# The first layer's high part of g: rounded by ScalarE in place of GpSimd

## The chip, the core and the metric

The kernel runs on one core of a Trainium2 chip. The time is the device time of one execution in microseconds; the core's engines are TensorE (PE, with PEld for its weight loads), VectorE (DVE), ScalarE (ACT), GpSimd (POOL) and SyncE (SP, which issues the DMAs). Each engine takes its own instructions in order and waits on semaphores for the others. The profile is one execution taken by the hardware profiler; its times count from the first instruction.

## The reference

Three parts follow one another: an attention in which a query sees only the keys of its own cluster, a dense layer (the first layer below), and a layer of four experts mixed by given probabilities (the second). The change lies in the first layer, on 1536 tokens:

```python
def _moe_ref(x, w_in, w_out):            # x [1536, 512], w_in [512, 2048], w_out [2048, 512]
    h = x @ w_in
    g = np.where(h > 0.0, h, 1.0 * (np.exp(np.minimum(h, 0.0)) - 1.0))
    return (g @ w_out).astype(np.float32)
```

`w_in` and `w_out` come in 64-bit floats; the kernel turns them into 32-bit ones itself.

## The kernel before

Every matrix product of the first layer is three matmuls of fp32r operands: a value x is split into a high part xh, which is x rounded to fp32r, and a low part xl = x - xh, and the products hh, hl and lh are summed in PSUM.

The layer is cut into 48 steps. A step takes one block of 512 tokens (`tb`, three of them) and one chunk of 128 of the 2048 columns of `w_in` (n, sixteen of them). The chunks form groups of 2, 4, 5 and 5; a group goes through all its chunks for one token block, then for the next. A step has two halves:

- `emit_G1(s)`: 12 matmuls (L745) make `h` in one of two PSUM buffers. ScalarE takes `r` = relu(-h) (L752) and exp(-r) (L753), VectorE joins them to `gg` (L754), and GpSimd splits `gg`: `gh` is its high part (L755), `gl` the low one (L756). `r` and `gg` have two buffers, `gh` and `gl` four.
- `emit_G2(s)`: 12 matmuls (L915) multiply `gh` and `gl` by the chunk's rows of `w_out` and add into four PSUM tiles `a`, of five buffers. At the end of a group the four tiles go to `acc` in SBUF: in the first group by four copies of ScalarE (L931), later by additions on VectorE (L933). The next step's second to fourth tile need the buffers that these free.

G1 runs two steps ahead of G2 (`LAG`): the program's order is G1(s+2), G2(s), G1(s+3), and so on. With G1(s+2) written before G2(s), the exp of step s+2 stands ahead of the L931 of step s in ScalarE's queue.

Between the two halves a clock of ticks moves generators on that load and split the weights of later chunks (`w_split`). A chunk takes from the 64-bit words: ScalarE L702 (absolute value of the high word) and L708 (its sign), VectorE L704, L707 and L710 (clamp, shift, join the words), ScalarE L714, VectorE L716 (the sign put back), ScalarE L718 (`wh`, the high part), GpSimd L721 (`wl`, the low part). L702 of one chunk waits until GpSimd has finished L721 of the chunk two before, whose buffer it takes. Chunks 0 and 1 are split during the attention, chunks 2 to 15 in the first layer; the last steps of the layer split what the second layer needs. In the second layer GpSimd has no work on `g`.

No line but one is touched; it stands in `emit_G1`.

Of the kernel before, what the change touches and what calls it, by code (L numbers as in the profile page):

```python
# [13 lines left out]
AF = mybir.ActivationFunctionType  # L14
ALU = mybir.AluOpType
# [31 lines left out]
def kernel(  # L47
# [14 lines left out]
    pe, act, dve, pool, sp = nc.tensor, nc.scalar, nc.vector, nc.gpsimd, nc.sync  # L62
# [661 lines left out]
    def moe():  # L724
# [10 lines left out]
        def emit_G1(s):  # L735
            ly, tb, n = steps[s][:3]
            if ly == 2:
                return
            wh, wl = w_t[n]
            ps = ps_h.tile([128, 512], F32, tag=f"h{s % 2}", name="h")  # L740
            for kk in range(KD):
                f = slice(kk * 128, (kk + 1) * 128)
                xh, xl = xT[tb][kk][:, 0], xT[tb][kk][:, 1]
                for i, (w, x) in enumerate(((wh, xh), (wh, xl), (wl, xh))):
                    pe.matmul(  # L745
                        ps, lhsT=w[:, 0, f], rhs=x, start=(kk == 0 and i == 0), stop=(kk == KD - 1 and i == 2)
                    )
            gh = gp.tile([128, 512], F32R, tag="gh", name="gh")
            gl = gp.tile([128, 512], F32R, tag="gl", name="gl")
            r = tp.tile([128, 512], F32, tag="r", name="r")  # L750
            gg = tp.tile([128, 512], F32, tag="gg", name="gg")
            act.activation(out=r, in_=ps, func=AF.Relu, scale=-1.0)  # L752
            act.activation(out=r, in_=r, func=AF.Exp, scale=-1.0)  # L753
            dve.scalar_tensor_tensor(out=gg, in0=r, scalar=-1.0, in1=ps, op0=ALU.add, op1=ALU.max)  # L754
            pool.tensor_scalar(gh, gg, 1.0, 0.0, ALU.mult, ALU.add)  # L755
            pool.tensor_tensor(gl, gg, gh.bitcast(F32), ALU.subtract)  # L756
            g_t[s] = [(gh, gl)]

# [238 lines left out]
        for s in range(-LAG, NS):  # L997


            nxt = s + (1 if s >= NS1 else LAG)  # L1000
            q = None
            if s < NS1:
                tick(2 * s)
            if nxt < NS1:
                emit_G1(nxt)
            elif nxt < NS and s != NS1 - 1:
                ready(nxt)
                q = quad_early(nxt)
            if s >= 0:
                emit_G2(s, (0,) if q else range(4))  # L1010
            if s < NS1:
                tick(2 * s + 1)
            if q:
                quad_late(nxt, *q)
                if s >= NS1:
                    tick(2 * s, 3)
                    tick(2 * s + 1, 2)
                emit_G2(s, (1, 2, 3))
            g_t.pop(s, None)
            if s == 12:  # L1020
                probs()
# [33 lines left out]
```

## Time and profile before

| | |
|---|---|
| three runs | 1055.17, 1059.05 (median), 1060.33 us |
| profiled execution, its time | 1059.59 us |
| its span, first to last instruction | 1057.9 us |
| granted TensorE clock, mean | 0.994 |
| busy: PE, DVE, ACT, POOL | 1033.5, 734.3, 525.0, 392.6 us |
| `gh` on POOL (L755), 48 instructions | 40.7 us, 849 ns each (615 to 1606) |
| `gl` on POOL (L756), 48 | 73.0 us, 1520 ns each (1286 to 2343) |
| `wl` on POOL (L721), 14 | 39.2 us, 2799 ns each |

The attention ends near 274 us, the first layer runs from there to 538 us, the second layer to the end. The mean times of GpSimd's instructions hide a spread: one shape takes anything between the two ends given. A clock of 1 is 2.4 GHz, 0.5 is 1.2 GHz. Busy matmuls overlap, so that a busy TensorE is told by the absence of idle time, not by its share.

### The profile page before, as it was taken

The page shows a single profiled execution, that of the slowest core. Times are in us where ns is not written, and L with a number is a line of the kernel's source. Part 1 is how long each engine was busy: PE and PEld are TensorE (multiplying, and loading weights), DVE is VectorE, ACT ScalarE, POOL GpSimd, SP SyncE. Part 2 cuts the span into 40 slices and gives each one's busy share as a digit, 9 for nine tenths or more (in the row PEclk, how much of TensorE's full clock was granted, in tenths as well). Part 3 has the DMA queues.
Part 4 walks back from the last instruction along what each step waited for, and adds up shares of the span by engine and source line. Part 5 has one row for each costly group of instructions (what it writes and reads, how often), then busy time and mean ns, then how long its engine had stood idle before and what let it go on. Part 6 is the DMA issues. An engine that isn't in the chain of part 4 may idle for free.

```text
span 1057.9 us, 16441 instructions
## 1 busy us (share of the span) xinstructions
PE 1033.5 (98%) x6253; PEld 922.4 (87%) x6253; DVE 734.3 (69%) x1248; ACT 525.0 (50%) x1081; POOL 392.6 (37%) x394
## 2 busy tenths in 40 slices
PE   7999999999989999999999999999999999999998
PEld 6999999989867888888888989898989898989897
DVE  6898999898658866244677666767666667666665
ACT  4889999888667654233443332333332333332331
POOL 2778888979568757353643000000000000000000
PEclk9899999999999999999999999999999999999999
DMA  7747554430332322010002001111011111011003
GB/s 176 170 119 162 129 126 119 125 89 7 118 118 83 118 79 82 0 40 1 1 1 81 11 30 40 41 40 40 6 36 40 40 41 40 3 38 41 1 1 120
DMA packets 61789, 67.53 MB, mean 64 GB/s; under 512 B 29008, under 2 KB 47440, under 8 KB 61712
## 3 DMA queue, kind: packets, MB, share of 16 engines
q1 hardware_dynamic: 61712, 66.49, 22.1%
q8 instruction: 49, 0.80, 0.3%
q14 instruction: 28, 0.23, 0.1%
HBM read 43.08 MB, written 3.15 MB: 44 GB/s over the span
## 4 chain that ended last, share of the span: by engine, by line
PE 81%; DVE 7%; POOL 4%; ACT 4%; issue 2%; SPq 1%; DMA 1%; POOLq 0%; ACTq 0%; DVEq 0%
PE a L915 35%; PE h L765 23%; PE h L745 10%; PE x L441 4%; PE tps L412 3%; PE s L364 2%; PE s L367 2%; POOL p L400 1%; DVE pl L433 1%; DVE nm L373 1%; SPq L228 1%; DVE wa L710 1%; DMA KB<-kh 1%; ACT e L382 1%; POOL wl L721 1%
## 5 line engine op out<-in xcount | busy, mean ns | idle before, releaser
L765 PEld LDWEIGHTS h<-x,w1op 128*128 128x128 f32 x2016 | 257.4, 190 | 10.2 <-ACT r L776 1.2
L765 PE MATMUL h<-x,w1op 128*128 128x256 f32 x2016 | 261.2, 285 | 1.0 <-ACT r L776 1.0
L915 PE MATMUL a<-w2op,gh 128*128 128x512 f32 x768 | 238.4, 392 | 0.0
L915 PEld LDWEIGHTS a<-w2op,gh 128*128 128x128 f32 x768 | 138.1, 188 | 23.8
L924 DVE SCALAR_TENSOR_TENSOR acc<-a,prob,acc 128x512 f32<-128x512 f32 x180 | 129.7, 747 | 40.1 <-PE a L915 40.1
L915 PE MATMUL a<-w2op,gl 128*128 128x512 f32 x384 | 149.8, 390 | 0.0
L745 PE MATMUL h<-xT,wh 128*128 128x512 f32 x384 | 119.0, 391 | 1.5 <-DVE gg L754 1.5
L400 POOL TENSOR_SCALAR p<-e,sm 128x768 f32<-128x768 f32 x96 | 88.4, 927 | 43.8 <-DVE sm L394 29.6
L754 DVE SCALAR_TENSOR_TENSOR gg<-r,h 128x512 f32<-128x512 f32 x48 | 32.9, 685 | 103.0 <-ACT r L753 81.5
L373 DVE TENSOR_REDUCE nm<-s 128x1 f32<-128x768 f32 x96 | 90.9, 947 | 4.3 <-PE s L367 4.1
L382 ACT ACTIVATE e<-s,nm 128x768 f32<-128x768 f32 x96 | 86.6, 902 | 3.9 <-POOL p L400 2.5
L412 PE MATMUL tps<-ident,p 128*128 128x128 f32 x576 | 85.3, 281 | 2.9 <-DVE pl L433 2.8
L745 PEld LDWEIGHTS h<-xT,wh 128*128 128x128 f32 x384 | 72.2, 189 | 17.3 <-DVE gg L754 2.3
L915 PEld LDWEIGHTS a<-w2op,gl 128*128 128x128 f32 x384 | 72.1, 188 | 15.7
L776 ACT ACTIVATE r<-h 128x256 f32<-128x256 f32 x48 | 18.4, 384 | 134.8 <-PE h L765 134.8
L433 DVE TENSOR_TENSOR pl<-tps,ph 128x512 fp32r<-128x512 f32 x112 | 76.2, 683 | 8.1 <-ACT ph L425 6.7
L915 PE MATMUL a<-gh,wh 128*128 128x512 f32 x192 | 75.5, 393 | 3.4 <-ACT acc L931 3.4
L441 PE MATMUL x<-ph,v 128*128 128x256 f32 x288 | 76.5, 297 | 1.4 <-DVE xs L461 1.3
L755 POOL TENSOR_SCALAR gh<-gg 128x512 fp32r<-128x512 f32 x48 | 40.7, 849 | 97.7 <-DVE gg L754 95.9
L915 PE MATMUL a<-gl,wh 128*128 128x512 f32 x192 | 75.4, 393 | 0.0
L915 PE MATMUL a<-gh,wl 128*128 128x512 f32 x192 | 75.2, 392 | 0.0
L745 PE MATMUL h<-xT,wl 128*128 128x512 f32 x192 | 74.8, 389 | 0.0
(152 smaller groups left out, 1900.3 us busy)
## 6 DMA issues: line engine op xcount, KB each, us to landing
st<-in_moe_w_dram SPq DMA_DIRECT2D x32, 512.0 KB, 4.3
st<-in_moe_w_in_dram SPq DMA_DIRECT2D x14, 512.0 KB, 3.7
st<-in_moe_w_out_dram SPq DMA_DIRECT2D x14, 512.0 KB, 4.6
QA<-qh SPq DMA_DIRECT2D x32, 192.0 KB, 4.0
nq<-in_q_dram SPq DMA_DIRECT2D x16, 192.0 KB, 3.8
nk<-in_k_dram SPq DMA_DIRECT2D x16, 192.0 KB, 3.8
nv<-in_v_dram SPq DMA_DIRECT2D x8, 384.0 KB, 4.1
QB<-ql SPq DMA_DIRECT2D x16, 192.0 KB, 4.2
```

Of the source, the lines that this page charges most:

```text
L373: dve.tensor_reduce(out=m_t[w][:, i:i + 1], in_=s_t[HALF * w + i][:, :, 0:384], axis=AX.XY, op=ALU.max, negate=True)
L382: act.activation(out=e, in_=s_t.pop(u)[:, :, 0:384], func=AF.Exp, bias=m_t[w][:, i:i + 1], accum_out=e_t[w][0][:, i:i + 1])
L400: pool.tensor_scalar(p, e_t[w][1 + i].rearrange("p a b -> p (a b)"), e_t[w][0][:, i:i + 1], 1.0, ALU.mult, ALU.mult)
L412: pe.transpose(ps[:, x, :], p_t[w][i][:, c * 128:(c + 1) * 128], ident)
L433: dve.tensor_tensor(out=l, in0=ps, in1=h.bitcast(F32), op=ALU.subtract)
L441: pe.matmul(x_t[w], lhsT=v2[j][:, r, c, :], rhs=t[:, :, c, :], start=(c == 0 and t is ph[w]), stop=(c == T - 1 and t is pl[w]),)
L745: pe.matmul(ps, lhsT=w[:, 0, f], rhs=x, start=(kk == 0 and i == 0), stop=(kk == KD - 1 and i == 2))
L754: dve.scalar_tensor_tensor(out=gg, in0=r, scalar=-1.0, in1=ps, op0=ALU.add, op1=ALU.max)
L755: pool.tensor_scalar(gh, gg, 1.0, 0.0, ALU.mult, ALU.add)
L765: pe.matmul(ps, lhsT=w[wz][kk], rhs=x[xz][:, kk], start=(start and kk + i == 0), stop=(stop and kk == 1 and i == 2), skip_group_check=True,)
L915: pe.matmul(ps, lhsT=x, rhs=y, start=(opens and i == 0), stop=(closes and i == len(ops) - 1))
L924: dve.scalar_tensor_tensor(out=t, in0=ps, scalar=pr, in1=t, op0=ALU.mult, op1=ALU.add)
```

## The change

ScalarE makes `gh` by a copy whose output type rounds; GpSimd keeps the subtraction. Both engines write the same tile from the same `gg`.

```diff
             act.activation(out=r, in_=ps, func=AF.Relu, scale=-1.0)
             act.activation(out=r, in_=r, func=AF.Exp, scale=-1.0)
             dve.scalar_tensor_tensor(out=gg, in0=r, scalar=-1.0, in1=ps, op0=ALU.add, op1=ALU.max)
-            pool.tensor_scalar(gh, gg, 1.0, 0.0, ALU.mult, ALU.add)
+            act.activation(out=gh, in_=gg, func=AF.Copy)
             pool.tensor_tensor(gl, gg, gh.bitcast(F32), ALU.subtract)
```

The order of the other instructions on every engine is the same before and after. On TensorE and VectorE nothing moves at all; on ScalarE 48 instructions come in, on GpSimd as many go.

ScalarE around the first L931, before (wh_4498 is the high part of chunk 3; L702 here belongs to chunk 4):

```order
L714 ACTIVATE wa<-wa 128x1024
L702 ACTIVATE wa<-st 128x1024
L752 ACTIVATE r<-h 128x512
L753 ACTIVATE r<-r 128x512
L931 ACTIVATE acc<-a 128x512 x4
L708 ACTIVATE wsg<-st 128x1024
L718 ACTIVATE wh_4498<-wa 128x1024
```

and with the change:

```order
L714 ACTIVATE wa<-wa 128x1024
L702 ACTIVATE wa<-st 128x1024
L752 ACTIVATE r<-h 128x512
L753 ACTIVATE r<-r 128x512
L755 ACTIVATE gh<-gg 128x512
L931 ACTIVATE acc<-a 128x512 x4
L708 ACTIVATE wsg<-st 128x1024
L718 ACTIVATE wh_4498<-wa 128x1024
```

The copy of the newest step has come between its exp and the four copies into `acc` of an older step.

ScalarE around the third L931, with the change (wh_4646 is the high part of chunk 5):

```order
L755 ACTIVATE gh<-gg 128x512
L708 ACTIVATE wsg<-st 128x1024
L718 ACTIVATE wh_4646<-wa 128x1024
L752 ACTIVATE r<-h 128x512
L753 ACTIVATE r<-r 128x512
L755 ACTIVATE gh<-gg 128x512
L931 ACTIVATE acc<-a 128x512 x4
L714 ACTIVATE wa<-wa 128x1024
```

The two L755 are new, the other rows stood there in this order before.

## Rows read from the trace of the kernel before

**Rows 1.** Busy by stretch: PE, PEld, DVE, ACT, POOL; PEclk, DMA, GB/s.
```profile
276.00:330.00 54.00, 49.10 (x204) 38.45 (x203) 35.66 (x31) 37.76 (x51) 33.87 (x22) 0.97 0.28 98
...
330.00:538.00 208.00, 208.00 (x919) 172.24 (x918) 119.76 (x136) 93.61 (x133) 126.57 (x95) 1.00 0.14 46
```

**Rows 2.** TensorE by time: start, length, operation; idle before, what ended it.
```profile
296.48 0.50 PE L915 MATMUL a<-gh,wh 128*128 128x512 f32 x1 [2.54 <-ACT acc L931]
...
317.92 0.74 PE L745 MATMUL h<-xT,wh 128*128 128x512 f32 x2 [0.91 <-DVE gg L754]
...
322.83 0.50 PE L915 MATMUL a<-gh,wh 128*128 128x512 f32 x1 [0.87 <-ACT acc L931]
...
325.69 0.73 PE L745 MATMUL h<-xT,wh 128*128 128x512 f32 x2 [0.55 <-DVE gg L754]
```

**Rows 3.** Busy by stretch, as rows 1 (PEclk third from the end).
```profile
296.48:303.00 6.52, 6.52 (x21) 5.22 (x22) 6.45 (x5) 4.64 (x7) 5.87 (x3) 0.74 0.00 0
```

**Rows 4.** The other three engines by time, 282 to 296 us.
```profile
282.75 0.67 DVE L754 SCALAR_TENSOR_TENSOR gg<-r,h 128x512 f32<-128x512 f32 x1
...
282.86 1.06 ACT L714 ACTIVATE wa<-wa 128x1024 f32<-128x1024 f32 x1 [1.55 <-DVE wa L710]
...
286.27 0.58 ACT L752 ACTIVATE r<-h 128x512 f32<-128x512 f32 x1
...
286.88 0.63 ACT L753 ACTIVATE r<-r 128x512 f32<-128x512 f32 x1
...
286.94 0.69 DVE L707 TENSOR_SCALAR wa<-wa 128x1024 int32<-128x1024 int32 x1
...
287.42 1.04 ACT L718 ACTIVATE wh<-wa 128x1024 fp32r<-128x1024 f32 x1
...
287.62 0.69 DVE L754 SCALAR_TENSOR_TENSOR gg<-r,h 128x512 f32<-128x512 f32 x1
...
288.23 1.22 DVE L710 SCALAR_TENSOR_TENSOR wa<-st,wa 128x1024 int32<-128x1024 int32 x1
...
288.40 1.53 POOL L755 TENSOR_SCALAR gh<-gg 128x512 fp32r<-128x512 f32 x1 [2.05 <-DVE gg L754]
...
290.01 1.29 POOL L756 TENSOR_TENSOR gl<-gg,gh 128x512 fp32r<-128x512 f32 x1
...
291.25 2.39 POOL L721 TENSOR_TENSOR wl<-wa,wh 128x1024 fp32r<-128x1024 f32 x1
...
293.68 1.12 ACT L702 ACTIVATE wa<-st 128x1024 f32<-128x1024 f32 x1 [3.14 <-POOL wl L721]
...
295.85 2.04 ACT L931 ACTIVATE acc<-a 128x512 f32<-128x512 f32 x4
```

**Rows 5.** ScalarE by time: a copy of 128x512 from SBUF to SBUF.
```profile
500.54 0.62 ACT L833 ACTIVATE x<-xs 128x512 fp32r<-128x512 f32 x1
```

**Rows 6.** The three engines by time, 319 to 325 us.
```profile
319.03 1.17 ACT L708 ACTIVATE wsg<-st 128x1024 f32<-128x1024 f32 x1 [1.96 <-DVE wa L716]
...
320.06 1.67 DVE L707 TENSOR_SCALAR wa<-wa 128x1024 int32<-128x1024 int32 x1
...
320.11 1.04 ACT L718 ACTIVATE wh<-wa 128x1024 fp32r<-128x1024 f32 x1
...
321.23 2.73 POOL L721 TENSOR_TENSOR wl<-wa,wh 128x1024 fp32r<-128x1024 f32 x1
...
321.76 3.28 DVE L710 SCALAR_TENSOR_TENSOR wa<-st,wa 128x1024 int32<-128x1024 int32 x1
...
322.19 2.04 ACT L931 ACTIVATE acc<-a 128x512 f32<-128x512 f32 x4
...
324.96 0.68 DVE L754 SCALAR_TENSOR_TENSOR gg<-r,h 128x512 f32<-128x512 f32 x1
```

**Rows 7.** ScalarE and VectorE by time, 308 to 318 us.
```profile
308.60 2.04 ACT L931 ACTIVATE acc<-a 128x512 f32<-128x512 f32 x4
...
317.17 0.69 DVE L754 SCALAR_TENSOR_TENSOR gg<-r,h 128x512 f32<-128x512 f32 x1 [6.62 <-ACT r L753]
```

## Prediction

> **What bounds the kernel now.** I read the busy time by stretch first. From 330 to 538 us, most of the first layer, TensorE is busy for all 208.00 us, while ScalarE is busy for 93.61 and GpSimd for 126.57: whatever moves between those two is covered there by matmuls, and costs nothing unless a step's ScalarE work outgrows the step [rows 1]. In the layer's opening, 276 to 330 us, TensorE is busy for 49.10 of 54.00 us [rows 1]. The missing 4.9 us are four waits in TensorE's rows: 2.54 before 296.48 and 0.87 before 322.83, both ended by the first copies into `acc` (L931), and 0.91 before 317.92 and 0.55 before 325.69, both ended by `gg` (L754) [rows 2]. The first wait also costs clock: over the 6.52 us from 296.48 to 303.00 the granted clock averaged 0.74 (it fell to half, 1.2 of 2.4 GHz, for part of it), so 0.26 x 6.52 = 1.7 us of work was lost [rows 3]. The change can only count in this opening, where ScalarE, VectorE and GpSimd split the weights of chunks 2 to 5 and work on `g` at once.
>
> **The change, part by part.** Removed: 48 copies on GpSimd; the one at 288.40 took 1.53 us [rows 4]. Added: 48 on ScalarE. The trace has a ScalarE copy of the same size and type, SBUF to SBUF: 0.62 us [rows 5]. Over 48 that is 30 us. Behind 330 us it lies under the matmuls, in the 208.00 - 93.61 = 114 us in which ScalarE is idle [rows 1]; if that cover were gone, each step would pay up to 0.62 + 0.69 (the wait for `gg`). Moved: nothing on TensorE, VectorE or the DMA queue (the loads of the weights only follow L710, which frees their buffers). But there is a new wait. ScalarE's `gh` needs `gg`, which VectorE makes after ScalarE's exp (L753). ScalarE, which takes its queue in order, thus stands still for `gg` (0.69) and then copies (0.62): everything queued behind comes 0.69 + 0.62 + 0.04 of hand-overs = 1.35 us later, later still if VectorE is late. What stands behind is L714, L718 (the weights) and, three times, L931, for which TensorE waits.
>
> One more thing from the rows: VectorE's operations on the weights and GpSimd's hold each other up. L710 took 1.22 us when it ran from 288.23 [rows 4], but 3.28 when GpSimd's `wl` ran from 321.23 to 323.96: it ended 1.08 after it [rows 6]. I treat them as taking turns, whoever asked first. `gg`, which reads PSUM, I take as free of this.
>
> I carry the rows forward to the three L931.
>
> *First.* `gg` of step 1 ends at 282.75 + 0.67 = 283.42; the copy behind it ends at 284.0, so L714 moves from 282.86 to 284.0 (+1.1) [rows 4]. The chunk's L716 and L708 and then step 2's L752 follow, the latter from 286.27 to 287.5 (+1.2) [rows 4]. `gg` of step 2 then ends at 289.5, its copy at 290.1, and L718 moves from 287.42 to 290.0, ending 291.05 [rows 4]. On GpSimd `gh` is gone, but `gl` must let L710 (1.22, from 289.5) pass: 290.7 + 1.29 = 292.0; `wl` 2.39 more: 294.4, against 291.25 + 2.39 = 293.64 [rows 4]. So the 1.53 taken off GpSimd is eaten up by the wait for L718, and `wl` is 0.7 late. L702 waits for it (293.68 to 294.4), L752 and L753 follow, and then the new `gg` and `gh` before L931: 295.85 + 0.7 + 1.35 = 297.9 [rows 4]. TensorE comes back about 2.05 us later, near 298.5.
>
> *Second.* The L931 at 308.60 moves by some 1.9 in the same way [rows 7]; TensorE, itself 2.05 late, meets it without a new wait. The L718 behind it is late by as much, but GpSimd is rid of `gh`, so `wl`, L702, L752 and `gg` at 317.17 come some 1.1 late: the latter ends at 319.0 [rows 7]. TensorE would have been there at 317.92 - 0.91 + 2.05 = 319.1. The 0.91 is swallowed, and its lag is 1.1 [rows 2].
>
> *Third.* Here the queue matters most. Before, L931 at 322.19 did not need the `gg` of its step, which ran only at 324.96 because VectorE stood in L710 [rows 6]. Now the copy of that `gg` stands ahead of L931. From 319.0: VectorE's L716 (1.2, as L710 of the same size) to 320.2; GpSimd's `gl` (1.29) to 321.5; L704 and L707 (0.6 to 0.7 each, as L707 alone took 0.69 [rows 4]) to 322.75. ScalarE after L716: L708 1.17, L718 1.04, ready at 322.4 [rows 6], so `wl` asks while L707 runs and goes first: 2.39, to 325.1; L710 ends 1.08 later at 326.2; `gg` 326.9; `gh` 327.5; the first L931 0.6 later, 328.1. TensorE restarts there instead of at 322.83: +5.3, after a wait of about 5.4 us [rows 2]. The 0.55 wait that followed falls away: lag 4.7.
>
> *Clock.* Nothing before shows so long a wait. Below: the waits of 0.87 and 0.91 left no such trace, so 0. Above: the 2.54 us wait cost 1.7 [rows 3]. 5.4 is nearer the latter, so I take 1.7. Behind 330 us TensorE has no wait to give the time back with [rows 1].
>
> Sum: 4.7 + 1.7 = 6.4 us. The profiled execution took 1059.59 (span 1057.9 and 1.7 around it), so 1066.0. The median of the three runs, 1059.05, lies 0.5 below the profiled execution, which is no more than the runs differ among themselves.
>
> **The rivals.**
> - *L710 goes first at the third place.* The margin in the sum is 0.35 us (322.4 against 322.75). Then L710 ends at 324.0, `gg` 324.7, `gh` 325.3, and TensorE restarts at 325.9: +3.1, less 0.55, plus 1.7 of clock: 4.25 us, 1063.8. For it: a small shift of ScalarE's L718 suffices. Against: at 321.23 the same turn fell to `wl` before [rows 6].
> - *A second drop, or the first one longer.* If the first wait, 4.6 instead of 2.54, cost another 1.7, and this lag were not swallowed at 317.92: 1067.7. For it: the longer the wait, the more the clock may fall [rows 3]. Against: at the second place TensorE waits for the other engines anyhow.
> - *Nothing comes of it.* If VectorE and GpSimd hinder each other less than I say, `wl` and L710 overlap, `gg` at the third place comes near 323.5, the lag stays under about 1.5 and there is no clock drop: 1059.6 to 1061.
> - *Faster.* GpSimd's `gh` no longer takes turns with VectorE: in the opening each copy takes up to 1.53 us out of their common time [rows 4]. If ScalarE's wait for `gg` is absorbed, the weights come sooner, and up to 4.9 us of waits and 1.7 of clock could go: 1053 at best, some 1056 likely. It decides if `wl` ends before 293.64 in spite of the later L718; in my sum it ends 0.7 after. The Trainium skill ("SBUF — State Buffer", section "Who interferes with whom") has the mechanism: a VectorE instruction with two SBUF inputs, or in a two-port mode, and a GpSimd instruction reading SBUF exclude each other for a whole instruction, and ScalarE never waits on anyone. By that page alone, moving a copy from GpSimd to ScalarE relieves a lock and should gain; the trace agrees on the lock (3.28 against 1.22), but the page's rule says nothing of ScalarE's queue.
>
> **How the numbers follow.** My forecast, `wl` first at the third place, gets 0.50 and 1066.0; L710 first 0.20 (1063.8); more clock lost 0.07 (1067.7); nothing 0.17 (1060); faster 0.06 (1056). Some 0.5%, 5.3 us, is what a measurement of this kernel tells from no change, so from 1059.6 the line lies at 1064.9. The forecast with 6.4 is barely over it, and about a fifth of its chance falls under; of L710 first a sixth falls over. Slower: 0.40 + 0.03 + 0.07 = 0.50; faster: 0.06; same: the rest, 0.44. The range takes in all of the two first cases, the upper end of "nothing" and most of the lost clock: 1060 to 1068.5.
>
> **What would show it.** In the profile after: `gh` on ScalarE near 0.62; at the first wait `acc` ending TensorE's idle time near 298.5 with over 4 us; no wait on `gg` near 319; a wait of 3 to 5.5 us for the third L931, with `gg` of that step just ahead of `gh`; half clock behind it; no TensorE wait from 335 to 538. The prediction is wrong if the third L931 comes within 1.5 us of TensorE's need, if `wl` comes sooner than before, or if waits arise behind 335 us, where I count none.

## The result, and the profile after

With the change the kernel takes 1068.01 us (median of five runs, 1064.69 to 1068.75), before it 1059.83 beside them: the ratio is 1.0075, with a 95% interval of 1.005 to 1.010. It is slower, by about 8 us. The profiled execution took 1068.1, its span 1066.3.

The page's first part, busy time by engine:

```profile
PE 1035.4 (97%) x6253; PEld 924.6 (87%) x6253; DVE 725.1 (68%) x1248; ACT 552.9 (52%) x1129; POOL 346.3 (32%) x346
```

The move itself is as announced: GpSimd lost 46 us and 48 instructions, ScalarE gained 28 us and 48. The group of the new line, with its idle time:

```profile
L755 ACT ACTIVATE gh<-gg 128x512 fp32r<-128x512 f32 x48 | 30.4, 633 | 48.6 <-DVE gg L754 48.6
```

So each copy takes 0.63 us and ScalarE stands still for `gg` 1.0 us ahead of it on average: the wait costs ScalarE more than the work. The stretches of [rows 1], and a later one that ends 2 us behind the first layer's new end at 543.78 (PE, PEld, DVE, ACT, POOL; PEclk, DMA, GB/s):

```profile
276.00:330.00 54.00, 44.90 (x181) 36.19 (x180) 28.23 (x27) 38.16 (x54) 21.75 (x13) 0.92 0.28 95
330.00:538.00 208.00, 208.00 (x916) 172.16 (x915) 112.19 (x132) 116.73 (x170) 89.88 (x54) 1.00 0.14 47
340.00:546.00 206.00, 205.37 (x912) 170.12 (x910) 112.09 (x134) 112.90 (x167) 87.99 (x55) 1.00 0.13 44
```

TensorE is idle for 9.1 of 54 us in the opening, against 4.9 in [rows 1]; the middle is still covered; 0.6 us is lost near 546. TensorE's rows at the waits, answering to [rows 2]:

```profile
298.51 0.80 PE L915 MATMUL a<-gh,wh 128*128 128x512 f32 x1 [4.44 <-ACT acc L931]
...
327.85 0.67 PE L915 MATMUL a<-gh,wh 128*128 128x512 f32 x1 [4.66 <-ACT acc L931]
...
546.45 0.74 PE L765 MATMUL h<-x,w1op 128*128 128x256 f32 x4 [1.08 <-ACT r L776]
```

Two waits of [rows 2] have grown (2.54 to 4.44, 0.87 to 4.66), two are gone (0.91, 0.55), and one at the end of the layer is new. The clock behind the two long ones, answering to [rows 3]:

```profile
298.51:305.00 6.49, 6.49 (x17) 5.13 (x18) 4.23 (x4) 5.70 (x9) 3.85 (x3) 0.57 0.27 77
327.85:335.00 7.15, 7.15 (x24) 5.76 (x25) 3.63 (x5) 6.29 (x10) 1.90 (x2) 0.76 0.35 128
```

It fell to half behind both, 1.2 of 2.4 GHz for part of the stretch. The first and third place on the other engines, where [rows 4] and [rows 6] show them before:

```profile
287.55 0.58 ACT L752 ACTIVATE r<-h 128x512 f32<-128x512 f32 x1
...
289.62 0.63 ACT L755 ACTIVATE gh<-gg 128x512 fp32r<-128x512 f32 x1 [0.82 <-DVE gg L754]
290.15 1.05 ACT L718 ACTIVATE wh<-wa 128x1024 fp32r<-128x1024 f32 x1
...
291.83 2.40 POOL L721 TENSOR_TENSOR wl<-wa,wh 128x1024 fp32r<-128x1024 f32 x1
...
294.26 1.12 ACT L702 ACTIVATE wa<-st 128x1024 f32<-128x1024 f32 x1 [2.11 <-POOL wl L721]
...
297.88 2.04 ACT L931 ACTIVATE acc<-a 128x512 f32<-128x512 f32 x4
...
322.51 2.46 POOL L721 TENSOR_TENSOR wl<-wa,wh 128x1024 fp32r<-128x1024 f32 x1 [1.03 <-PE h L745]
...
322.79 3.25 DVE L710 SCALAR_TENSOR_TENSOR wa<-st,wa 128x1024 int32<-128x1024 int32 x1
...
325.97 0.68 DVE L754 SCALAR_TENSOR_TENSOR gg<-r,h 128x512 f32<-128x512 f32 x1
...
326.68 0.63 ACT L755 ACTIVATE gh<-gg 128x512 fp32r<-128x512 f32 x1 [3.11 <-DVE gg L754]
327.22 2.04 ACT L931 ACTIVATE acc<-a 128x512 f32<-128x512 f32 x4
```

At the third place one reads the chain from below: TensorE waits for L931, L931 stands behind `gh`, `gh` waited 3.11 us for `gg`, and `gg` stands behind an L710 that took 3.25 us beside GpSimd's `wl`.

At the layer's end (ScalarE and VectorE, 541 to 547 us):

```profile
541.98 1.51 DVE L660 TENSOR_TENSOR T<-st 128x256 f32<-128x256 f32 x1
543.41 0.41 DVE L661 TENSOR_TENSOR T<-st 128x256 f32<-128x256 f32 x1
543.75 0.68 DVE L754 SCALAR_TENSOR_TENSOR gg<-r,h 128x512 f32<-128x512 f32 x1
...
544.46 0.64 ACT L755 ACTIVATE gh<-gg 128x512 fp32r<-128x512 f32 x1 [1.94 <-DVE gg L754]
545.00 0.61 ACT L833 ACTIVATE x<-xs 128x512 fp32r<-128x512 f32 x1
545.51 0.61 ACT L645 ACTIVATE w1op<-st 128x512 fp32r<-128x512 f32 x1
546.03 0.36 ACT L776 ACTIVATE r<-h 128x256 f32<-128x256 f32 x1
```

The same pattern once more: the last `gh` waits 1.94 us for a `gg` behind VectorE's other work, and ScalarE comes to L776, the second layer's first relu, without a pause and too late for TensorE. In the trace of before it had idled there for 1.13 us:

```profile
537.23 0.62 ACT L645 ACTIVATE w1op<-st 128x512 fp32r<-128x512 f32 x1
538.98 0.38 ACT L776 ACTIVATE r<-h 128x256 f32<-128x256 f32 x1 [1.13 <-PE h L765]
```

**A ledger.** Single runs of one kernel differ by some 5 us, so I add up profiled executions by stretch: the first layer (first L745 to first L765), the second (to the end of the last matmul), and the rest of the span. Before 264.03 + 515.89 + 3.95, after 269.62 + 517.52 + 5.00: +5.59, +1.63, +1.05, together 8.3, against 8.5 between the two profiled times (1068.1 - 1059.59). Two marks go further into the opening: when TensorE begins G2 of step 6, ahead of the third place (46.78 us after the first L745 before, 48.19 after), and G1 of step 10, behind it (57.31 and 62.90). From there to the layer's end both need 206.72 us.

### The profile page after: what moved, and what is told of

It reads as the page before. It is cut to its first block, busy times and chain, and to the rows that moved or that the text cites. A ratio compares the mean times of both kernels' runs of the same rounds, so it can differ in the third digit from the quotient of the medians.

```text
span 1066.3 us, 16427 instructions
## 1 busy us (share of the span) xinstructions
PE 1035.4 (97%) x6253; PEld 924.6 (87%) x6253; DVE 725.1 (68%) x1248; ACT 552.9 (52%) x1129; POOL 346.3 (32%) x346
## 4 chain that ended last, share of the span: by engine, by line
PE 80%; DVE 7%; ACT 5%; POOL 3%; issue 3%; SPq 1%; DMA 0%; ACTq 0%; POOLq 0%; DVEq 0%
PE a L915 34%; PE h L765 23%; PE h L745 9%; PE x L441 4%; PE tps L412 4%; PE s L364 2%; PE s L367 2%; DVE pl L433 1%; POOL p L400 1%; DVE nm L373 1%; ACT e L382 1%; POOL wl L721 1%; ACT ph L425 1%; PE lps L240 1%; PE lps L239 1%
## 5 line engine op out<-in xcount | busy, mean ns | idle before, releaser
L765 PEld LDWEIGHTS h<-x,w1op 128*128 128x128 f32 x2016 | 257.5, 190 | 11.8 <-ACT r L776 2.8
L765 PE MATMUL h<-x,w1op 128*128 128x256 f32 x2016 | 261.6, 285 | 2.2 <-ACT r L776 2.1
L915 PE MATMUL a<-w2op,gh 128*128 128x512 f32 x768 | 238.4, 392 | 0.0
L915 PEld LDWEIGHTS a<-w2op,gh 128*128 128x128 f32 x768 | 138.1, 188 | 23.9
L915 PE MATMUL a<-w2op,gl 128*128 128x512 f32 x384 | 149.8, 390 | 0.0
L745 PE MATMUL h<-xT,wh 128*128 128x512 f32 x384 | 118.9, 391 | 0.0
L756 POOL TENSOR_TENSOR gl<-gg,gh 128x512 fp32r<-128x512 f32 x48 | 67.4, 1403 | 149.2 <-ACT gh L755 141.7
L754 DVE SCALAR_TENSOR_TENSOR gg<-r,h 128x512 f32<-128x512 f32 x48 | 32.9, 686 | 102.6 <-ACT r L753 102.5
L776 ACT ACTIVATE r<-h 128x256 f32<-128x256 f32 x48 | 18.4, 383 | 134.0 <-PE h L765 134.0
L745 PEld LDWEIGHTS h<-xT,wh 128*128 128x128 f32 x384 | 72.6, 189 | 15.3
L915 PEld LDWEIGHTS a<-w2op,gl 128*128 128x128 f32 x384 | 72.1, 188 | 15.6
L915 PE MATMUL a<-gh,wh 128*128 128x512 f32 x192 | 76.3, 398 | 9.1 <-ACT acc L931 9.1
L915 PE MATMUL a<-gl,wh 128*128 128x512 f32 x192 | 76.1, 397 | 0.0
L915 PE MATMUL a<-gh,wl 128*128 128x512 f32 x192 | 76.0, 396 | 0.0
L745 PE MATMUL h<-xT,wl 128*128 128x512 f32 x192 | 75.0, 390 | 0.0
```

The source lines that it names most:

```text
L745: pe.matmul(ps, lhsT=w[:, 0, f], rhs=x, start=(kk == 0 and i == 0), stop=(kk == KD - 1 and i == 2))
L765: pe.matmul(ps, lhsT=w[wz][kk], rhs=x[xz][:, kk], start=(start and kk + i == 0), stop=(stop and kk == 1 and i == 2), skip_group_check=True,)
L915: pe.matmul(ps, lhsT=x, rhs=y, start=(opens and i == 0), stop=(closes and i == len(ops) - 1))
```

## Experiments

All numbers in one table (us; the marks count from the first L745; the end is the span, which the profile gives to a tenth, less the end of the last matmul). "Before" was run beside each, with medians of 1059.03 to 1059.41; the recorded ratio is not exactly the quotient of the two medians.

| | median | ratio, 95% interval | first layer | second | end | G2(6) | G1(10) |
|---|---|---|---|---|---|---|---|
| before | 1059.83 | | 264.03 | 515.89 | 3.95 | 46.78 | 57.31 |
| the change | 1068.01 | 1.0075 [1.0050, 1.0100] | 269.62 | 517.52 | 5.00 | 48.19 | 62.90 |
| E1 steps below 10 | 1065.22 | 1.0045 [1.0028, 1.0062] | 269.63 | 516.19 | 3.96 | 48.11 | 62.91 |
| E2 steps from 10 | 1061.86 | 1.0027 [1.0018, 1.0037] | 264.05 | 517.24 | 5.05 | 46.77 | 57.33 |
| E3 steps 3, 5, 7 | 1063.87 | 1.0037 [1.0023, 1.0051] | 269.23 | 515.91 | 3.89 | 46.63 | 62.51 |
| E4 all but 3, 5, 7 | 1063.21 | 1.0030 [1.0014, 1.0046] | 265.49 | 517.53 | 5.00 | 48.47 | 58.77 |
| E5 step 7 | 1065.11 | 1.0059 [1.0040, 1.0078] | 269.12 | 516.18 | 3.93 | 46.74 | 62.40 |
| E6 step 3* | 1058.74 | 1.0003 [0.9979, 1.0027] | 262.90 | 516.18 | 3.93 | 46.75 | 56.17 |
| E7 fillers | 1066.41 | 1.0070 [1.0039, 1.0100] | 268.06 | 517.52 | 5.07 | 47.95 | 61.34 |
| E8 all but the last 3 | 1065.93 | 1.0066 [1.0029, 1.0104] | 270.83 | 516.19 | 4.19 | 47.95 | 64.11 |
| E9 tiny copies* | 1056.02 | 0.9992 [0.9974, 1.0010] | 264.06 | 515.91 | 3.88 | 46.78 | 57.34 |
| E10 third buffer | 1053.85 | 0.9958 [0.9944, 0.9972] | 258.60 | 515.90 | 3.91 | 42.45 | 51.88 |
| E11 change, third buffer* | 1062.02 | 1.0028 [1.0012, 1.0044] | 266.56 | 517.37 | 3.86 | 45.25 | 59.84 |
| E12 change, behind L931 | 1061.66 | 1.0024 [1.0006, 1.0042] | 264.13 | 517.49 | 5.06 | 47.24 | 57.41 |

The profiled executions marked * began the first layer 3.5 to 3.7 us sooner than the one of before (at 270.31 to 270.50 us against 274.03); the stretches and marks count from there and can be compared with the others.

In E1 to E6 and E8 the copy (L755) runs on ScalarE in some steps and on GpSimd, as before, in the others; in each the edit is this one line. E1 is

```diff
-            pool.tensor_scalar(gh, gg, 1.0, 0.0, ALU.mult, ALU.add)
+            act.activation(out=gh, in_=gg, func=AF.Copy) if s < 10 else pool.tensor_scalar(gh, gg, 1.0, 0.0, ALU.mult, ALU.add)
```

**E1, the opening alone.**

> ScalarE rounds g for steps 0 to 9 only, GpSimd for steps 10 to 47. Theory (the copies queue ahead of L931 in the opening): TensorE's waits in the opening as with the whole change, 4.4 and 4.7 us with a dropped clock behind both; the lag at the first matmul of the second layer's product about 5.6 us, and no wait on ScalarE's r there beyond that of before; time 5.5 to 7 us over before. Rival (ScalarE's 48 copies cost in proportion, wherever they are): 10 of 48 of the 8 us, under 2 us.

The first layer is 5.60 us longer, as with the whole change, and the other stretches stay within 0.3 of before. The opening's share is settled: 5.6.

**E2, the rest alone.**

```diff
+            act.activation(out=gh, in_=gg, func=AF.Copy) if s >= 10 else pool.tensor_scalar(gh, gg, 1.0, 0.0, ALU.mult, ALU.add)
```

> ScalarE rounds g for steps 10 to 47 only, GpSimd for steps 0 to 9. Theory: the opening is that of before (waits of 2.5, 0.9, 0.9, 0.6 us); what is left is the wait of 1.1 us for the first r of the second layer, with some tenths; time 1 to 2 us over before. Rival (cost in proportion): 38 of 48 of the 8 us, 6 to 7 us over before.

The opening is as before; the second stretch is 1.35 longer (the wait on L776 stands in it, 1.07) and 1.1 are lost behind the last matmul. The 38 copies that I had put down at nothing cost 2.5 us. With E1's 5.6 that makes 8.1 of the ledger's 8.3.

**E3, E4, E5, E6: which copies of the opening.** Steps 3, 5 and 7 are those whose copy stands ahead of an L931. The four lines below are those of E3, E4, E5 and E6, in this order.

```diff
+            act.activation(out=gh, in_=gg, func=AF.Copy) if s in (3, 5, 7) else pool.tensor_scalar(gh, gg, 1.0, 0.0, ALU.mult, ALU.add)
+            act.activation(out=gh, in_=gg, func=AF.Copy) if s not in (3, 5, 7) else pool.tensor_scalar(gh, gg, 1.0, 0.0, ALU.mult, ALU.add)
+            act.activation(out=gh, in_=gg, func=AF.Copy) if s == 7 else pool.tensor_scalar(gh, gg, 1.0, 0.0, ALU.mult, ALU.add)
+            act.activation(out=gh, in_=gg, func=AF.Copy) if s == 3 else pool.tensor_scalar(gh, gg, 1.0, 0.0, ALU.mult, ALU.add)
```

> ScalarE rounds g only in steps 3, 5 and 7, whose copies stand directly ahead of the three L931. Theory (place in the queue): L931 comes 1.35 us later at the first place, 1.4 at the second, and at the third waits for the late gg of its step, so a wait of 3.5 to 5 us there; lag behind the opening 4 to 5.5 us; time 4 to 6 us over before. Rival (the copies make the weights late, through L714 and L718 behind them, and that is what TensorE waits for): three copies of ten, 1.5 us at most.

> ScalarE rounds g in all steps but 3, 5 and 7. Theory (place in the queue): L931 no longer waits for the gg of its step; the first L931 comes 0.7 us late because wl is late, the third about 1.5 us late; TensorE waits under 3.5 and under 2.5 us; lag behind the opening 0 to 2 us, with 1.3 at the start of the second layer; time 1 to 3 us over before. Rival (weights late): nearly as slow as the whole change, 6 to 8 us over before.

> ScalarE rounds g in step 7 alone, whose copy stands ahead of the third L931. Theory (the third place sets the lag, since gg of step 7 comes late and the earlier waits are swallowed): one copy of 48 brings most of it, a wait of 3.5 to 5 us at the third place with a dropped clock, and a lag of 4.5 to 5.5 us at the first matmul of the second layer's product, against 5.6 with all copies. Rival (the lag adds up over the three places): about a third, 1.4 to 2 us.

> ScalarE rounds g in step 3 alone, whose copy stands ahead of the first L931. Theory: the first wait is 1.4 us longer (3.9 us), but the wait for gg before the third token block's first chunk takes that back, so a lag under 1 us remains. Rival (adds up): the 1.4 us remain, with any clock lost on top, 1.4 to 3 us.

E3 gives 5.2 of the 5.6 us at G1(10), E4 1.5. They do not add up, for two reasons. TensorE that comes late to a place waits less there (E6, below). And E4 meets a slow L710 that the whole change does not meet:

```profile
300.42 3.30 DVE L710 SCALAR_TENSOR_TENSOR wa<-st,wa 128x1024 int32<-128x1024 int32 x1
...
304.35 0.63 ACT L755 ACTIVATE gh<-gg 128x512 fp32r<-128x512 f32 x1 [3.36 <-DVE gg L754]
...
310.31 0.50 PE L915 MATMUL a<-gh,wh 128*128 128x512 f32 x1 [1.53 <-ACT acc L931]
```

There the copy of step 4 waits 3.36 us for its `gg`, the weights' L714 stands behind it, and TensorE waits for the second L931. With the whole change the same copy waited 0.76, and this wait is not there. E5 is the sharpest: one instruction of 0.63 us on another engine costs 5.1. TensorE's, ScalarE's, VectorE's and GpSimd's rows of E5:

```profile
320.36 2.71 POOL L721 TENSOR_TENSOR wl<-wa,wh 128x1024 fp32r<-128x1024 f32 x1
...
320.90 3.26 DVE L710 SCALAR_TENSOR_TENSOR wa<-st,wa 128x1024 int32<-128x1024 int32 x1
...
324.08 0.67 DVE L754 SCALAR_TENSOR_TENSOR gg<-r,h 128x512 f32<-128x512 f32 x1
...
324.79 0.63 ACT L755 ACTIVATE gh<-gg 128x512 fp32r<-128x512 f32 x1 [3.36 <-DVE gg L754]
325.32 2.04 ACT L931 ACTIVATE acc<-a 128x512 f32<-128x512 f32 x4
...
325.95 0.79 PE L915 MATMUL a<-gh,wh 128*128 128x512 f32 x1 [4.85 <-ACT acc L931]
```

Here nothing ahead of the third place was late, and the wait is as long. E6 lengthens the first wait to 4.00 us, and costs nothing:

```profile
294.40 0.50 PE L915 MATMUL a<-gh,wh 128*128 128x512 f32 x1 [4.00 <-ACT acc L931]
```

G2(6) comes at 46.75 as before, since the waits of 0.91 and 0.87 in [rows 2] vanish from its trace. What is lost at the first place is swallowed at the second. (Behind it E6 gains 1.1 at the third place, where its 0.87 is missing too. Its ratio shows no gain.)

**E7, the clock.** The whole change, with 17 matmuls into an unused PSUM buffer in each of the two long waits. Their result goes nowhere.

```diff
+        def fill(n, tb):
+            z = ps_h.tile([128, 512], F32, tag="h2", name="z")
+            for _ in range(17):
+                pe.matmul(z, lhsT=w_t[n][0][:, 0, 0:128], rhs=xT[tb][0][:, 0], start=True, stop=True)
...
+                if s in (2, 6) and m == 1: fill(n, tb)
```

> The whole change, with 17 matmuls more in steps 2 and 6, right before the matmul that waits for L931; they multiply tiles that are there already into a PSUM tile that nobody reads, and keep TensorE busy for 3.9 us of the waits of 4.4 and 4.7 us. Theory (part of the lag is the dropped clock): TensorE restarts at the same times as with the whole change, the granted clock stays at 1.0 behind both, and the lag is 1.5 to 2 us less than 5.6. Rival (the clock costs nothing here, since the other engines set the pace): the same lag, within 0.3 us.

The clock stays whole:

```profile
296.48:303.00 6.52, 5.93 (x26) 4.58 (x25) 5.48 (x6) 5.70 (x9) 3.14 (x2) 1.00 0.04 10
326.00:334.00 8.00, 6.92 (x31) 5.57 (x31) 3.30 (x6) 7.03 (x11) 1.91 (x2) 1.00 0.40 133
```

TensorE at the second and third place (L921 and L937 are L915 and L931 in this kernel):

```profile
310.62 0.50 PE L921 MATMUL a<-gh,wh 128*128 128x512 f32 x1 [1.50 <-ACT acc L937]
...
327.28 0.50 PE L921 MATMUL a<-gh,wh 128*128 128x512 f32 x1 [1.08 <-ACT acc L937]
```

The layer is 1.56 us shorter than with the change, and all of it comes from the third place. TensorE goes on there 53.73 us after the first L745, with the change 53.69; from there to G1(10) it needs 7.61 us, with the change 9.21. So the half clock behind the third wait costs 1.6. The one behind the first costs next to nothing in the end: without it TensorE comes sooner to the second L931 and waits 1.50 us for it. The price behind the third place differs among executions: the same stretch took 9.20 us in E1, 9.62 in E5, 10.19 in E3 and 10.41 in E8. The ratios do not tell the 1.6 us from nothing (1.0070 and 1.0075, with intervals that overlap).

**E8, without the layer's last three copies.**

```diff
+            act.activation(out=gh, in_=gg, func=AF.Copy) if s < 45 else pool.tensor_scalar(gh, gg, 1.0, 0.0, ALU.mult, ALU.add)
```

> The whole change but for the last three steps (45 to 47), in which GpSimd rounds g as before. Theory (at the end of the layer the copy, late for its gg, stands ahead of the copies for the second layer and of its first r): the wait of 1.1 us for the first r of the second layer goes, and what lies between the first matmul of its product and the last matmul shrinks by 1.1 to 1.4 us; the opening stays at 5.6. Rival (ScalarE is late there for another reason, such as a backlog from the whole layer): the wait stays.

The wait on L776 is gone and the second stretch is back at 516.19; this execution lost more to the clock at the third place (0.54 from 327.85 to 335, against 0.76 with the change), hence its long first layer. The late wait is the doing of those three copies.

**E9, only the number of ScalarE's instructions.** The kernel before, with 38 copies of a tile of 128x1 (`tiny`, filled once ahead of the layer) more on ScalarE.

```diff
+            if s >= 10: act.activation(out=tiny, in_=tiny, func=AF.Copy)
```

> The kernel before, with GpSimd's rounding kept, plus 38 ScalarE copies of 128x1 behind the low part of g from step 10 on (and one that fills their input); the added work is not part of the computation. They take well under 0.3 us each and wait for nothing that comes late. Theory (the later landing of the last output goes with the number of ScalarE's instructions alone): last matmul to the end of the span 4.9 to 5.1 us against 3.95, 29 or 30 transfers in the instruction queue against 28, the opening and the second layer unchanged within 0.3 us, no TensorE wait near 546; profiled execution about 1060.6. Rival (it goes with what the added copies of g do to the end of the layer): 3.9 to 4.0 us behind the last matmul, 28 transfers, 1059.6.

The end is 3.88 us, as before, so the theory falls: 38 more instructions do not make it. The transfers in the instruction queue rose by one; but E10 and E11 have 30 of them, as E2 has, and ends of 3.91 and 3.86. More on the end stands below.

**E10 and E11, a third buffer for the weights.** L702 waits for GpSimd's `wl` of the chunk two before, whose buffer it takes; with three buffers it need not. The first is the kernel before with this line, the second the change with it.

```diff
-        a32, sg = tmp if small else [gtile(("qh", "kl")[n % 2], "wa", [128, 2, 512], I32), gtile("ql", "wsg", [128, 2, 512], I32)]
+        a32, sg = tmp if small else [gtile(("qh", "kl", "kh")[n % 3], "wa", [128, 2, 512], I32), gtile("ql", "wsg", [128, 2, 512], I32)]
```

> The kernel before with a third buffer for the weights in the split, so that ScalarE's L702 of a chunk no longer waits for GpSimd's wl of the chunk two before. Theory (the first wait hangs on that buffer: L702 waited 3.14 us for wl, and L752, L753 and L931 stand behind it): L702 of chunk 4 starts near 290.5 instead of 293.68, the first L931 near 293, the 2.54 us wait and its half clock go: the opening 2.5 to 4.5 us shorter, 1055 to 1057. Rival (VectorE and GpSimd together set the pace of the weights, so that the buffer only lets ScalarE run ahead and the waits at the second and third place grow by as much): 1059 to 1060.

> The change with the third buffer for the weights. Theory (the first wait hangs on that buffer, the third on ScalarE's copy of g that stands ahead of the third L931 behind VectorE's L710): the first wait of 4.44 us shrinks under 2, the third one stays or grows, because it no longer meets a TensorE that is late already: 4 to 7 us; opening 1 to 3 us shorter than with the change, 1065 to 1067. Rival (both waits hang on the buffer): both gone, opening as before or shorter, 1060 to 1062.

E10 is the fastest kernel of the study, with a ratio of 0.9958 (0.9944 to 0.9972); its first layer is 5.4 us shorter than before, more than I expected. Its stretch of the opening, and its ScalarE at the first place:

```profile
276.00:330.00 54.00, 52.42 (x228) 41.87 (x227) 40.81 (x34) 41.49 (x56) 39.33 (x25) 1.00 0.31 104
```

```profile
290.41 1.11 ACT L702 ACTIVATE wa<-st 128x1024 f32<-128x1024 f32 x1
...
292.58 2.04 ACT L931 ACTIVATE acc<-a 128x512 f32<-128x512 f32 x4
```

L702 starts 3.3 us sooner than in [rows 4], L931 too; the first wait and the half clock of [rows 3] are gone. TensorE has two waits left:

```profile
306.11 0.50 PE L915 MATMUL a<-gh,wh 128*128 128x512 f32 x1 [0.92 <-ACT acc L931]
...
320.23 0.73 PE L745 MATMUL h<-xT,wh 128*128 128x512 f32 x2 [0.55 <-DVE gg L754]
```

The second is the last of [rows 2]; the first is new, for the second L931. In E11 the first wait shrank to 2.22, not under 2; a second one of 1.59 came up and the third was 3.79, a little under my 4. With three buffers the change costs 7.96 us at G1(10) (59.84 against 51.88): more than with two. That less waiting is left to swallow it (1.47 us in E10, 4.87 in [rows 2]) fits, and so does the clock, which is whole in E10 and 0.67 from 320 to 328 us in E11; neither was tested by itself. The first layer is 3.1 us shorter than with the change (266.56 against 269.62), at the end of my 1 to 3, and the span's end 1.1 shorter. Of the rival, that both waits hang on the buffer, only the time came true (1062), not the reason; my own time, 1065 to 1067, did not.

**E12, the same copies behind L931.** The whole change, but in steps 3, 5 and 7 `gh` and `gl` are written behind the four copies into `acc`, so that their order in ScalarE's queue is swapped. (`split` holds the two lines that write them, `later` is a list; the lines that set these up are left out here.)

```diff
+            if s in (3, 5, 7):
+                later.append(split)
+            else:
+                split()
...
                 emit_G2(s, (0,) if q else range(4))
+            while later:
+                later.pop()()
```

> The whole change, on the same engine, but in steps 3, 5 and 7 the copy of g (and the low part that needs it) is written behind the step's four copies into acc, so that ScalarE passes only L931 ahead of it. Theory (the third wait is ScalarE's queue: gh stands ahead of L931 and waits for gg behind L710): L931 starts right behind its step's exp, the third wait falls from 4.66 to 0.5 to 2 us, the first from 4.44 to 2.5 to 3.4, the clock keeps full behind the third place; first layer 264.5 to 267 us long against 264.03 before and 269.62 with the change, profiled execution 1062.5 to 1065.5 with the 2.4 us that the change loses at the layer's end and behind the last matmul. Rival (the copies delay the weights, whatever stands ahead of L931): third wait still over 3.5 us, 268.5 to 269.6, 1067 to 1068.

ScalarE and VectorE at the third place (L937 is L931 in this kernel, L757 is L755, L755 is L754), and TensorE's row there (L921 is L915):

```profile
321.62 3.28 DVE L710 SCALAR_TENSOR_TENSOR wa<-st,wa 128x1024 int32<-128x1024 int32 x1
...
322.32 2.04 ACT L937 ACTIVATE acc<-a 128x512 f32<-128x512 f32 x4
...
322.95 0.50 PE L921 MATMUL a<-gh,wh 128*128 128x512 f32 x1 [1.15 <-ACT acc L937]
...
325.53 0.63 ACT L757 ACTIVATE gh<-gg 128x512 fp32r<-128x512 f32 x1 [1.17 <-DVE gg L755]
```

L710 still takes 3.28 us and `gg` is as late, but L931 no longer stands behind it. The wait is 1.15, the clock stays at 1.00 from 326 to 335, and the first layer is 264.13 us long, 0.1 more than before. The first wait is 2.98 against 4.44. In the opening's trace the order of instructions on VectorE and GpSimd is that of the change; only ScalarE's differs, in these three places. So all 5.6 us hang on the order in ScalarE's queue, not on the engine that rounds. What is left of the ratio (1.0024) is the 1.6 and 1.1 behind the opening.

## Why the prediction came out as it did

The direction and the place were right; the size came from two errors that partly cancelled: 6.4 us were predicted for the opening and 5.6 measured, 0 for the rest and 2.7 measured. That 1068.01 lies inside 1060 to 1068.5 is in part luck: with the rest added to a right mechanism of the predicted size, 1059.59 + 6.4 + 2.7 would have been 1068.7.

*First place.* The replay held to 0.2 us: L714 283.89 (284.0 predicted), L752 287.55 (287.5), L718 290.15 (290.0), the end of `wl` 294.2 (294.4), L931 297.88 (297.9), TensorE back at 298.51 (298.5). The half clock behind it was longer, 0.57 over 6.49 us against 0.74 over 6.52 in [rows 3], which the prediction had kept as it was.

*Second place.* The 0.91 was swallowed as said, and E6 shows how. The lag ahead of the third place was 1.4 (48.19 - 46.78), not 1.1: at G2 of step 3 TensorE was 2.89 late (31.87 us after the first L745, against 28.98), and 1.48 of it were swallowed. Which copies make this lag stays open: E3 has none there (46.63), E4 1.7, but E12, which keeps all 48 copies, only 0.5 (47.24).

*Third place.* `wl` went first with a margin of 0.28 us (322.51 against 322.79; 0.35 predicted), L931 came at 327.22, TensorE at 327.85 (328.1), after 4.66 us. (The 5.4 of the prediction is a slip: by its own figures TensorE comes at 322.83 - 0.87 + 1.1 = 323.1 and waits 5.0.) The 0.55 fell away. E5 and E12 confirm the step that carried the prediction, that `gh` stands ahead of L931 behind a slow L710. The clock fell as assumed; its price is 1.6 by E7, where the sum had 1.7. Counted from the first L745, TensorE goes on at 53.69 us instead of 48.80, 4.9 later where the sum had 5.3; and the 8.51 us from there to G1(10) before, against 7.61 in E7, gave back 0.9 where it had 0.55. So the term of 4.7 + 1.7 measured 4.0 + 1.6 = 5.6.

*The step that failed* is that nothing behind the opening counts; "if waits arise behind 335 us, where I count none" was one of the prediction's own signs of being wrong, and one arose (1.08 us at 546.45). From 330 to 538 the cover held (208.00 of 208.00 us). But with [rows 1] I had looked at the layer's busy middle and applied it to all 38 copies, and the last three lie where the split of the second layer's weights crowds VectorE and a chain to its first relu begins: 1.3 us by E8. The other missing term, 1.05 us behind the last matmul, has no place in the prediction at all.

*The rivals.* L710 did not go first. The first clock drop was longer, but without it (E7) TensorE goes on at the third place no sooner. "Nothing" needed `wl` and L710 to overlap freely, and L710 took 3.25 us beside `wl`. Against "faster" the trace says that the relief is real and of no use: L710's mean fell from 2.07 to 1.93 us and VectorE's busy time by 9.2. The Trainium skill ("SBUF — State Buffer", section "Who interferes with whom") tells of the lock behind this; the trace agrees (L710 3.25 us where `wl` had started first, 1.22 in [rows 4], where no `wl` ran), but such a rule prices an overlap, and what decided was a queue.

*The end.* The last store is issued at the same distance from the last matmul, 0.82 us (before and after):

```profile
1054.76 0.33 SPq L927 DMA_DIRECT2D out_dram<-acc  x1
```

```profile
1062.12 0.33 SPq L927 DMA_DIRECT2D out_dram<-acc  x1
```

From there to the end of the span it is 3.14 us before and 4.18 after. What grew is the time until the store lands. Of all the stores of this line (before and after):

```profile
DMA to landing us min/median/max: 2.0/2.0/2.1
```

```profile
DMA to landing us min/median/max: 2.0/2.0/3.2
```

The trace lists single transfers too. With the change one of the instruction queue starts 2.65 us behind the last matmul, while the store is under way. So it is in every kernel with an end of 5.0 to 5.1 (the change, E2, E4, E7, E12), and their last store lands 3.2 us after its issue. In the nine others no such transfer starts between the last matmul and 4.5 us behind it, and the last store lands after 2.0 us. (E8's 4.19 does not come from its store: VectorE's last instruction comes late there.) So the end goes with the moment at which an instruction transfer falls, not with the number of ScalarE's instructions (E9) or of the transfers. Whether this transfer holds the store up, and why it falls there, stays open: no run tested it.

## What to carry to other kernels

Before an operation is moved to a less busy engine, read which instruction it will stand in front of there, and what it will itself wait for: in the opening its own 0.63 us cost next to nothing, its place ahead of L931 cost 5.6 us, and moving it behind L931 brought them back. Where a stretch is covered, look at its two ends apart from its middle, since the next stage's first instructions wait in the same queue. And where a wait of the bounding engine goes back to a buffer, try one more buffer first: that was worth some 5 us here (0.9958).

## What the runs showed of the hardware

Losses at successive places are not added: a first wait lengthened by 1.46 us (E6), with a half clock behind it, left no trace 20 us later, since TensorE would have waited there anyhow. The clock fell to half behind waits of 4.4 to 4.9 us with TensorE idle, and stayed at 1.00 in E7, where it worked on matmuls that nobody needs. It fell behind the 2.54 us of [rows 2] too (0.74), and did not behind 2.22 us in E11 (1.00 from 292.44 to 300) or behind 1.07 and 1.15 us in E12. A last store landed 2.0 us after its issue in nine kernels, and 3.2 us in the five in which an instruction transfer ran beside it.
